# Later due times for two weight splits in a gated attention and MLP kernel on one core

## The chip, the cores and the metric

The kernel runs on one NeuronCore of a Trainium2 chip, on engines that each work through a queue of their own: TensorE (PE, matmuls, with its weight loads shown as PEld), VectorE (DVE), ScalarE (ACT), GpSimd (POOL), and SyncE (SP), which issues the DMAs. The metric is the device time of one execution in microseconds (us), as the median of several runs.

## The reference

The input x has 2048 tokens of 448 features. The result is a gated mix of a sliding-window attention and an MLP, all in float32:

```python
x = A_x
g = _sigmoid((x * gate_w).sum(-1, keepdims=True))
a = _A_ref(x, A_wqkv, A_wo)
b = _B_ref(x, B_w1, B_b1, B_w2, B_b2)
return g * a + (1 - g) * b
```

Attention has 16 heads of 28 features; each token attends to 8 earlier tokens, itself included, 2 apart. The MLP goes from 448 to 1792 features (w1), squares the positive part, and goes back to 448 (w2).

## The kernel before

**Float32 by splitting.** A matmul here multiplies in a shorter format (F32R). Every operand is split into a high part ("hi": a ScalarE copy into the shorter format) and a low part ("lo": a VectorE subtraction, raw minus hi), and a product is the sum of three matmuls, hi·hi, hi·lo and lo·hi. The weights of the MLP must be loaded, split, and kept.

**Row halves and turns.** Most matmuls use 64 rows of the array, two side by side on the two row halves, and collect in PSUM banks. When a bank has had products of one row half and is to have those of the other, something must stand between: `turn` and `turned` write one element of the bank on VectorE (lines 212 and 360), and `touch` rewrites a few weights or activations on ScalarE (line 814). Each waits for the matmuls before it, and the matmuls behind it wait for it.

**Stages.** The tokens come in four chunks of 512. The first part of the program computes q, k and v of the chunks: `qkv_first` (chunk 0, 36 full matmuls that count as 36 pairs, then 48 and 42 pairs), `qkv_two` twice for chunk 1 (63 pairs each), `qkv_seven` for chunk 2 (117 pairs in groups of three, a scheme with seven products, its banks named v, x, y, z, w), and `qkv_two` twice for chunk 3. The second call for chunk 3 has the first MLP matmuls in it (`mlp_one` behind pair 51, `mlp_two` behind pair 57). Its `run` lists the steps by pairs: 24, turn q0,k1; 30, turn q1,k0; 42, turn v0,v1; 45, evacuate q0,k1; 51, `mlp_one`; 54, evacuate q1,k0; 57, `mlp_two`; 63, evacuate v0,v1. After it the MLP runs to the end, with attention on GpSimd and VectorE beside it and its output projection in between.

**The planner.** The order of the instructions on every engine is written by hand, through a clock. `advance(dt)` adds the planned time of the matmuls just issued (203 ns for a pair of 448 columns, 227 ns for one of 512), then issues every step whose due time has come, in order of due time, and then the attention pieces that are due. `when(t, ...)` registers a step for the absolute planned time t, `at(dt, ...)` one for dt from now. `run` advances by up to 12 pairs at once; `beside` and `go` by three. So a due time says only at which of these points a step is issued. Engines execute in the order of issue: a step whose data isn't there holds all that stands behind it on its engine.

**The steps that are moved.** `w1_piece(1, dt, gap)` loads a quarter of w1 at 45,500 and splits it in four parts, part k due at dt + k·gap, with `split_full` (line 130 hi, line 131 lo 1500 ns later); the fourth part consists of four smaller ones. `w2_piece(0, 4, t, gap)` loads four of the 14 row blocks of w2 at 85,500 (the DMA is line 792) and splits block k at t + k·gap with `split_copied`: ScalarE writes hi (745) and copies the raw block to one PSUM tile named copy (746); VectorE's low (751) is due 1300 ns (COPY_DELAY) later and reads that tile, so the next block's copy waits for it. `w2_piece(4, 3, ...)` does so for three more blocks. PSUM has two rings of four banks, "m" and "b"; a new tile takes the bank that was taken longest ago, and waits until that one has been read.

Of the kernel before, what the change touches and what calls it, by code (L numbers as in the profile page):

```python
# [57 lines left out]
def gated_mix_kernel(ctx: ExitStack, tc: tile.TileContext, xT, wqkv, w1, w2, wo, b1, b2, out):  # L58
# [868 lines left out]
    def when(t, fn, *args):  # L927
        later.append((t, lambda: fn(*args)))
# [117 lines left out]
    when(10500.0, x_spill, 0, x)  # L1046
    when(25000.0, w1_piece, 0, 38000.0, 1500.0)
    when(44500.0, halos)
    when(45500.0, w1_piece, 1, 57300.0, 1200.0)
    when(66800.0, w1_piece, 2, 76300.0, 1400.0)  # L1050
    when(67800.0, w1_piece, 3, 83500.0, 900.0)
    for j in range(2):
        when(65500.0 + j * 2000.0, x_copy, 3, j)
    when(78500.0, biases)
    when(85500.0, w2_piece, 0, 4, 91000.0, 1400.0)
    when(89100.0, w2_piece, 4, 3, 99700.0, 1400.0)

    pair = {}
# [442 lines left out]
```

## Time and profile before

| | |
|---|---|
| median of 3 runs | 415.39 us (415.28 to 415.41) |
| the profiled execution | 415.74 us |
| its span, first to last instruction | 414.0 us |
| granted TensorE clock | 1.00 |
| TensorE waits inside the span, two for a turn | 2.0 and 0.7 us |
| DMA | 74.00 MB, 179 GB/s on average |

The timeline lists instructions of an engine: start (us from the start of the span), duration, engine, line of the kernel, operation, what it writes and reads, shapes, how many of them the row merges (x4), and in brackets the idle time of the engine before it and what ended that. A start may lie a little (some 0.07 us) before the end of the instruction ahead, since they overlap. The list of waits names who waited for whom, with the total, the number of times, and the longest. The list of DMA issues has the queue, the size of one and the time from issue to landing.

### The profile page before, as it was taken

The page shows a single profiled execution, that of the slowest core. Times are in us where ns is not written, and L with a number is a line of the kernel's source. Part 1 is how long each engine was busy: PE and PEld are TensorE (multiplying, and loading weights), DVE is VectorE, ACT ScalarE, POOL GpSimd, SP SyncE. Part 2 cuts the span into 40 slices and gives each one's busy share as a digit, 9 for nine tenths or more (in the row PEclk, how much of TensorE's full clock was granted, in tenths as well). Part 3 has the DMA queues.
Part 4 walks back from the last instruction along what each step waited for, and adds up shares of the span by engine and source line. Part 5 has one row for each costly group of instructions (what it writes and reads, how often), then busy time and mean ns, then how long its engine had stood idle before and what let it go on. Part 6 is the DMA issues. An engine that isn't in the chain of part 4 may idle for free.

```text
span 414.0 us, 9366 instructions
## 1 busy us (share of the span) xinstructions
PE 407.1 (98%) x3817; PEld 367.6 (89%) x3817; DVE 278.8 (67%) x454; ACT 218.5 (53%) x494; POOL 268.0 (65%) x167
## 2 busy tenths in 40 slices
PE   8999999998999999999999999999999999999997
PEld 8999998997888888888888888989898888888996
DVE  4574865483876767787665888788686676784344
ACT  4674776474775466444465525544652254346640
POOL 0000000964999999989899799899899797850000
DMA  7999799979263505554022628965155630058504
GB/s 218 346 376 332 239 367 282 368 233 332 72 211 152 207 2 180 207 186 152 2 83 76 227 97 239 254 187 155 25 170 187 228 129 0 25 138 160 127 2 179
DMA packets 67020, 74.00 MB, mean 179 GB/s; under 512 B 33504, under 2 KB 59296, under 8 KB 66848
## 3 DMA queue, kind: packets, MB, share of 16 engines
q1 hardware_dynamic: 66976, 73.39, 55.6%
q8 instruction: 30, 0.49, 0.5%
q14 instruction: 14, 0.11, 0.1%
HBM read 45.94 MB, written 28.25 MB: 179 GB/s over the span
## 4 chain that ended last, share of the span: by engine, by line
PE 95%; DMA 2%; DVE 1%; ACT 0%; issue 0%; DVEq 0%
PE b L202 32%; PE h L202 32%; PE qkv L202 14%; PE a L202 7%; DMA w2raw<-w 2%; PE v L344 2%; PE qkv L291 2%; PE x L344 1%; PE z L344 1%; PE warm L879 1%; PE a L1273 1%; PE y L344 1%; PE w L344 0%; DVE st L437 0%; DVE w17l L131 0%
## 5 line engine op out<-in xcount | busy, mean ns | idle before, releaser
L561 POOL TENSOR_TENSOR qk<-q,k 128x896 f32<-128x896 f32 x64 | 135.0, 2150 | 86.3 <-DMA k<-k_d 77.3
L568 POOL TENSOR_TENSOR av<-lg,v 128x896 f32<-128x896 f32 x64 | 119.3, 1969 | 5.1 <-DVE lg L562 4.8
L866 DVE TENSOR_TENSOR h<-h,h 128x512 fp32r<-128x512 f32 x56 | 38.5, 689 | 60.8 <-ACT h L869 60.7
L576 DVE TENSOR_REDUCE o<-av 128x112 f32<-128x896 f32 x64 | 66.7, 1074 | 0.4 <-POOL av L568 0.3
L562 DVE TENSOR_REDUCE lg<-qk 128x32 f32<-128x896 f32 x64 | 66.9, 1075 | 0.0
L202 PE MATMUL b<-w2ah,h 64*128 64x448 f32 x448 | 66.3, 359 | 0.0
L202 PE MATMUL b<-w2bh,h 64*128 64x448 f32 x448 | 66.1, 359 | 0.0
L202 PE MATMUL qkv<-wqh,x 64*128 64x448 f32 (+1 forms) x384 | 60.9, 361 | 2.0 <-DVE qkv L212 2.0
L867 ACT ACTIVATE h<-h,b1z 128x512 f32<-128x512 f32 x56 | 36.7, 656 | 42.8 <-PE h L202 42.8
L202 PEld LDWEIGHTS qkv<-wqh,x 64*128 64x128 f32 x384 | 45.4, 184 | 3.8 <-DVE qkv L212 2.3
L202 PEld LDWEIGHTS b<-w2bh,h 64*128 64x128 f32 x448 | 42.1, 184 | 3.6
L202 PE MATMUL qkv<-wql,x 64*128 64x448 f32 (+1 forms) x192 | 45.2, 361 | 0.0
L202 PEld LDWEIGHTS b<-w2ah,h 64*128 64x128 f32 x448 | 41.9, 184 | 3.7
L202 PE MATMUL b<-w2bl,h 64*128 64x448 f32 x224 | 40.6, 358 | 0.0
L202 PE MATMUL b<-w2al,h 64*128 64x448 f32 x224 | 40.5, 358 | 0.0
L868 ACT ACTIVATE h<-h 128x512 fp32r<-128x512 f32 x56 | 33.5, 599 | 1.7
L869 ACT ACTIVATE h<-h 128x512 f32<-128x512 f32 x56 | 33.2, 593 | 0.0
L814 ACT ACTIVATE h<-h 128x4 fp32r<-128x4 f32 (+1 forms) x35 | 7.2, 207 | 43.9 <-PE b L202 41.5
L243 ACT ACTIVATE st<-qkv 128x448 f32<-128x448 f32 x36 | 18.2, 542 | 16.4 <-PE qkv L202 12.9
L202 PEld LDWEIGHTS qkv<-wql,x 64*128 64x128 f32 x192 | 25.8, 185 | 0.8
L202 PEld LDWEIGHTS b<-w2bl,h 64*128 64x128 f32 x224 | 21.1, 184 | 1.9
L202 PEld LDWEIGHTS b<-w2al,h 64*128 64x128 f32 x224 | 21.0, 184 | 1.9
(263 smaller groups left out, 851.7 us busy)
## 6 DMA issues: line engine op xcount, KB each, us to landing
k<-k_d SPq DMA_DIRECT2D x8, 840.0 KB, 6.6
v<-v_d SPq DMA_DIRECT2D x8, 840.0 KB, 4.8
x_d<-x SPq DMA_DIRECT2D x12, 512.0 KB, 7.7
q_d<-st SPq DMA_DIRECT2D x8, 448.0 KB, 6.6
k_d<-st SPq DMA_DIRECT2D x8, 448.0 KB, 6.4
w1raw<-w SPq DMA_DIRECT2D x4, 896.0 KB, 10.1
q<-q_d SPq DMA_DIRECT2D x8, 448.0 KB, 3.7
o_d<-o SPq DMA_DIRECT2D x16, 224.0 KB, 2.2
```

The costliest lines, as they stand in the source:

```text
L202: nc.tensor.matmul(acc.pt[:, :acc.n], a[rows], w[rows], start=acc.todo == acc.all, stop=acc.todo == 1)
L243: nc.scalar.activation(st[:, :, t % 2], heads(pt), AF.Copy)
L291: nc.tensor.matmul(acc.pt[:, :D], a, w, start=k == j == 0, stop=False)
L344: nc.tensor.matmul(self.pt[:, :self.n], a, w, start=new, stop=True, skip_group_check=True)
L561: nc.gpsimd.tensor_mul(pr, q[:, s:s + 1].to_broadcast([P, W, C]), k[:, s:s + W])
L562: pending.append(lambda: nc.vector.tensor_reduce(lg[:, s], pr.rearrange("p w (h d) -> p w h d", h=HG), axis=AX.X, op=ALU.add))
L568: nc.gpsimd.tensor_mul(pr.rearrange("p (h d) w -> p w h d", h=HG), lg[:, s][:, :, :, None].to_broadcast([P, W, HG, DH]), v[:, s:s + W].rea ...
L576: nc.vector.tensor_reduce(o[:, g * C:(g + 1) * C], pr, axis=AX.X, op=ALU.add)
L866: nc.vector.tensor_sub(hl, pt, f32(hh))
L867: ops += [lambda pt=pt, r=r: nc.scalar.activation(pt, pt, AF.Relu, bias=b1t[:, f + r:f + r + 1]), lambda pt=pt, hh=hh: nc.scalar.activatio ...
L868: lambda pt=pt, hh=hh: nc.scalar.activation(hh, pt, AF.Square),
L869: lambda pt=pt, r=r, low=low: (nc.scalar.activation(pt, pt, AF.Square), at(delays[r], low))]
```

## The change

Two due times and gaps. The first block of the second MLP weights is split from 93,200 in steps of 1500 instead of from 91,000 in steps of 1400, and the second piece of the first MLP weights from 58,000 in steps of 1300 instead of from 57,300 in steps of 1200. The loads stay where they are, and no instruction is added or removed.

```diff
@@ -1046,13 +1046,13 @@
     when(10500.0, x_spill, 0, x)
     when(25000.0, w1_piece, 0, 38000.0, 1500.0)
     when(44500.0, halos)
-    when(45500.0, w1_piece, 1, 57300.0, 1200.0)
+    when(45500.0, w1_piece, 1, 58000.0, 1300.0)
     when(66800.0, w1_piece, 2, 76300.0, 1400.0)
     when(67800.0, w1_piece, 3, 83500.0, 900.0)
     for j in range(2):
         when(65500.0 + j * 2000.0, x_copy, 3, j)
     when(78500.0, biases)
-    when(85500.0, w2_piece, 0, 4, 91000.0, 1400.0)
+    when(85500.0, w2_piece, 0, 4, 93200.0, 1500.0)
     when(89100.0, w2_piece, 4, 3, 99700.0, 1400.0)
```

## The prediction

> **What bounds the kernel now.** I began with the engine shares, then the list of who waited for whom on TensorE.
>
> ```profile
> PE 407.1 (98%) x3817; PEld 367.6 (89%) x3817; DVE 278.8 (67%) x454; ACT 218.5 (53%) x494; POOL 268.0 (65%) x167
> ```
>
> ```profile
> PE qkv L202 <- DVE qkv L212: 2.0, 1, 2.0
> ...
> PE x L344 <- DVE w L360: 0.7, 1, 0.7
> ```
>
> TensorE sets the time. Beside its start it waits twice, each time for a VectorE memset that turns a bank: a 1x1 write to one PSUM bank, which must stand between matmuls of one row half and those of the other. The timeline of TensorE gives the places:
>
> ```profile
> 66.52 0.36 PE L344 MATMUL x<-w2ah,s_0h 64*128 64x448 f32 x1
> ...
> 70.00 0.47 PE L344 MATMUL x<-w2ah,s_0h 64*128 64x448 f32 x2 [0.65 <-DVE w L360]
> ...
> 100.85 0.36 PE L202 MATMUL qkv<-w7h,x 64*128 64x450 f32 x2
> 103.17 0.47 PE L202 MATMUL qkv<-wqh,x 64*128 64x448 f32 x2 [1.95 <-DVE qkv L212]
> 103.48 0.37 PE L202 MATMUL qkv<-wql,x 64*128 64x448 f32 x2
> ...
> 106.28 0.40 PE L202 MATMUL h<-x,w17h 64*128 64x512 f32 x2
> ...
> 110.27 0.39 PE L202 MATMUL h<-x,w1ah 64*128 64x512 f32 x2
> ```
>
> From 103.48 to 106.28 run 14 pairs, so a pair takes 2.80 / 14 = 0.20 us. Gap two: the next pair was due at 100.85 + 0.20 = 101.05 and began at 103.17, 2.12 late; the pair behind it lost 0.11 more (0.31 instead of 0.20), together **2.2 us**. Gap one: 12 pairs after 66.52 is 68.92, the start was 70.00, 1.08 late, with the same loss at the restart **1.2 us**. So 3.4 us is all that can be taken out here.
>
> **Where the edited steps stand.** The kernel's planner adds 203 ns per qkv pair and releases due steps after at most 12 pairs (3 in the third chunk and the MLP). The third chunk starts at 252 pairs, 51,156 ns; the second half of the fourth at 126 + 126 + 117 + 63 = 432 pairs, 87,696 ns. I call its points by pairs: 24 (92,568), 30 (93,786), 42 (96,222), 45 (96,831), 51 (98,049), then twelve MLP pairs of 227 ns ending at 100,773, then 54 (101,382). Banks q0,k1 are turned after 24, q1,k0 after 30, v0,v1 after 42; q0 and k1 are evacuated after 45. Before, at 24: split 0, low 0, split 1, one reduction, then the turn. VectorE shows this:
>
> ```profile
> 101.42 0.62 DVE L751 TENSOR_TENSOR w2al<-copy,w2ah 128x448 fp32r<-128x448 f32 x1 [6.84 <-ACT copy L746]
> 101.96 1.08 DVE L562 TENSOR_REDUCE lg<-qk 128x32 f32<-128x896 f32 x1
> 102.97 0.64 DVE L751 TENSOR_TENSOR w2al<-copy,w2ah 128x448 fp32r<-128x448 f32 x1
> 103.03 0.64 DVE L212 MEMSET qkv<- 1x1 f32 x4
> ...
> 104.76 2.07 DVE L562 TENSOR_REDUCE lg<-qk 128x32 f32<-128x896 f32 x2
> ```
>
> VectorE idled 6.84 us in front of low 0 with two turns queued behind it. ScalarE shows why:
>
> ```profile
> 100.37 0.58 ACT L745 ACTIVATE w2ah<-w2raw 128x448 fp32r<-128x448 f32 x1 [4.99 <-DMA w2raw<-w]
> 100.86 0.53 ACT L746 ACTIVATE copy<-w2raw 128x448 f32<-128x448 f32 x1
> 101.32 0.56 ACT L745 ACTIVATE w2ah<-w2raw 128x448 fp32r<-128x448 f32 x1
> 102.08 0.55 ACT L746 ACTIVATE copy<-w2raw 128x448 f32<-128x448 f32 x1 [0.20 <-DVE w2al L751]
> ...
> 105.37 0.96 ACT L243 ACTIVATE st<-qkv 128x448 f32<-128x448 f32 x2
> ...
> 109.25 0.21 ACT L814 ACTIVATE w1ah<-w1ah 128x2 fp32r<-128x2 f32 x1 [1.26 <-PE h L202]
> ```
>
> The split waits for the load, landed at 100.35. All splits of this piece go through one PSUM copy tile: each copy (L746) waits for the low (L751) of the row before, as at 102.08.
>
> **Part one, the second weights.** Same 4 splits and 4 lows, no new instruction, no DMA moved (the load is still released by 85,500). New due times: splits 93,200 / 94,700 / 96,200 / 97,700, lows 1300 later. Split 0 goes to point 30; low 0, split 1, low 1 and split 2 to point 42 (96,200 just makes 96,222), low 2 and split 3 to 51, low 3 into the MLP pairs. Turns q0,k1 and q1,k0 now have no low ahead, and run when their matmuls are done. The turn v0,v1 gets low 0 and low 1 ahead.
>
> So gap two goes. What is late next: **the evacuation of q0**. It stands on ScalarE behind copy 2, which waits for low 1, and the MLP's first pair needs its bank. The "m" ring has four banks; the fourth chunk takes three (q0, q1, k0), then three (q0, q1, k1), so the two MLP tiles get the older k0's bank and this q0's. The chain, from the rows above:
> - load 100.35; hi 0 100.37; copy 0 100.86 to 101.39; low 0 101.42 to 102.04 (its reduction has run long before)
> - copy 1 102.08 to 102.63; low 1, 0.03 later (as copy 1 follows low 0), 102.66 to 103.29 (no reduction stands between: those of point 42 come behind the due steps)
> - copy 2 103.32 to 103.87; evacuation of q0 from 103.80 (it overlaps by 0.06, as at 105.37), 0.54 us, to 104.34; TensorE 0.05 later, **104.39**.
>
> Before, this pair began at 106.28, on no wait. Without either gap it would come at 106.28 - 3.4 = 102.9, with gap two alone gone at 104.1. Both are ahead of 104.39, so a new wait of 0.3 to 1.5 us stands there, and the gain is 106.28 - 104.39 = 1.89, less up to 0.1 for the restart: **1.8 us**.
>
> What follows it. Turn v0,v1: low 1 to 103.29, two reductions of 1.08, so 105.4; needed 9 pairs of this mix behind 104.39, at about 107.7: covered. The ScalarE touch of line 814, which frees the second MLP pass: low 2 to 105.8, copy 3 to 106.4, a reduction to 106.8, low 3 to 107.4, the next piece's copy to 108.0, touch to 108.15. TensorE wants it at 110.27 - 1.89 = 108.38: covered by 0.2 us only. If that cover fails the gain is what is left of 110.27 - 108.15 = 2.1, so each further reduction in this queue would cost 1.08 - 0.2 = 0.9 us.
>
> The load's landing is the anchor. It is issued at 90.74 behind a key load that waits for GpSimd, not TensorE:
>
> ```profile
> 90.74 0.39 SPq L792 DMA_DIRECT2D w2raw<-w  x1
> ...
> 95.80 1.20 SPq L792 DMA_DIRECT2D w2raw<-w  x1
> ```
>
> ```profile
> w2raw<-w SPq DMA_DIRECT2D x1, 896.0 KB, 9.6
> ...
> w2raw<-w SPq DMA_DIRECT2D x1, 672.0 KB, 10.2
> ...
> q_d<-st SPq DMA_DIRECT2D x1, 448.0 KB, 8.9
> ```
>
> If gap one goes, the stores of q and k behind the load are issued 1.2 us earlier. At worst they take half of the transfer for that time, and it lands 0.6 us later; at best nothing changes. The q store landed at about 92.7 + 8.9 = 101.6, behind the load, which is nearer to no change; I take 0 and keep 0.6 for the range.
>
> The Trainium skill, page "DMA: Bandwidth & Descriptors", section "Queues, rings and completion order", says that each DMA engine consumes the descriptors of one issuing queue in ring order, and that completion is nevertheless not first-in, first-out. By ring order the sum stays at 1.8, by free interleaving it would be 1.2; the landings at 100.35 and 101.6 agree with the first.
>
> **Part two, the first weights.** Old and new due times of the four splits: 57,300 / 58,500 / 59,700 / 60,900 and 58,000 / 59,300 / 60,600 / 61,900; lows 1500 behind the point of release. Before, the last low (four pieces) came ahead of the turn of x:
>
> ```profile
> 66.43 0.63 DVE L131 TENSOR_TENSOR w1al<-w1raw,w1ah 128x448 fp32r<-128x448 f32 x1 [1.13 <-ACT w1ah L130]
> 66.98 1.15 DVE L437 TENSOR_TENSOR st<-y,st 128x448 f32<-128x448 f32 x2
> 68.04 0.61 DVE L131 TENSOR_TENSOR w1al<-w1raw,w1ah 128x448 fp32r<-128x448 f32 x1
> 68.69 1.17 DVE L131 TENSOR_TENSOR w17l<-w1raw,w17h 64x64 fp32r<-64x64 f32 x4
> 69.86 0.06 DVE L360 MEMSET x<- 1x1 f32 x2
> ```
>
> ```profile
> 64.96 0.98 ACT L433 ACTIVATE st<-x 128x448 f32<-128x448 f32 x2 [0.79 <-DMA q_d<-st]
> 65.82 1.05 ACT L130 ACTIVATE w1ah<-w1raw 128x448 fp32r<-128x448 f32 x2
> 66.89 1.26 ACT L130 ACTIVATE w17h<-w1raw 64x64 fp32r<-64x64 f32 x4
> 68.06 0.95 ACT L433 ACTIVATE st<-z 128x448 f32<-128x448 f32 x2
> ```
>
> After, low 2 is released at 62,727 ahead of the turn of x and low 3 at 63,945 behind it, ahead of the turn of w. ScalarE: hi 1 and hi 2 still at 65.82, then the evacuation of z, now ahead of the four pieces: at 67.1 at the earliest, at 68.06 as before at the latest (it had no wait there). VectorE: the two adds start between 65.94 (x evacuated) and 66.98 as before, I take 66.4; 1.15 later low 1, then low 2 to 68.7, turn of x at 68.7; with the late end 69.3, which would leave 0.4 us of gap one. TensorE needs it at 68.92: gap one goes, with 0.2 us to spare. Turn of w: the pieces end 0.95 + 1.26 behind the start of z's evacuation, at 69.3 to 70.3, low 3 0.3 later; needed 9 pairs behind 68.92, at 70.7, so covered by 0.1 us at least. The raw buffer is released at 69.6 to 70.6 instead of 69.86; the load that waits for it on SP's queue is split some 20 us later. It all gives 1.2 us to TensorE at 70, which **wait again at 104.39**, because that chain hangs on a landing: I cost part two at 0 in the sum. Were the evacuation not in the way, it would be worth its 1.2.
>
> **Behind 110 us.** TensorE has no wait there, so it carries the gain on unless something not tied to it is late. GpSimd:
>
> ```profile
> 97.47 2.13 POOL L561 TENSOR_TENSOR qk<-q,k 128x896 f32<-128x896 f32 x1
> 103.12 2.13 POOL L561 TENSOR_TENSOR qk<-q,k 128x896 f32<-128x896 f32 x1 [3.52 <-DVE qkv L212]
> ```
>
> It waited for the reduction behind low 0. That reduction now runs ahead of the lows, so the product starts at 97.47 + 2.13 = 99.6. The mask step behind it waits for the first of the two reductions that stood at 104.76 (end 105.80) and now follow low 1 (end 104.3): it comes 1.5 us earlier, close to TensorE's 1.8. The last projection reads of attention are landed long before their split:
>
> ```profile
> 369.90 1.38 SPq L1205 DMA_DIRECT2D ot<-o_d  x2
> ```
>
> ```profile
> DMA to landing us min/median/max: 2.8/3.5/5.9
> ```
>
> ```profile
> 380.12 0.83 ACT L1222 ACTIVATE oh<-ot 128x768 fp32r<-128x768 f32 x1
> ```
>
> At the longest landing of such reads (the second fence) the data is there at 371.3 + 5.9 = 377.2, 2.9 us ahead of the split. On ScalarE the splits of piece two press on the MLP's first evacuations and the touch near 115; I see 0 to 0.2 us there and leave it in the range.
>
> **The sum**: 1.8 us. The profiled execution took 415.74 us (span 414.0), the median of the runs shown is 415.39; taken off the median, 415.39 - 1.8 = **413.6 us**; 413.9 with a span of 412.2 for the profiled one.
>
> **Rivals.**
> - *The bank isn't held*, or the chain is quicker than I have it. Then the touch bounds (2.1 us, 413.3), or in the extreme both gaps go whole (3.4 us, 412.0). For it: no row shows a wait for q0's evacuation yet. Against it: the order on ScalarE follows from the due times, and both bounds hang on the same landing.
> - *The queue fills again*: the landing comes 0.6 later and one more reduction (0.9) falls ahead of the touch: 1.8 - 0.6 - 0.9 = 0.3 us, 415.1, which is within 0.2% (0.8 us, about what a measurement of this kernel can tell from no change). For it: covers of 0.2 us.
> - *Slower*: ScalarE stands in front of the touch with the first split of piece two, whose load landed at 95.80 + 10.2 = 106.0. A hi, a copy and the touch behind it take about 1.35 us. If the load lands behind 108.9, the second MLP pass starts later than 110.27, microsecond for microsecond: a landing at 110 would give 416.5. For it: stores issued earlier share its transfer. Against: it needs 2.9 us more than before.
> - *The edits don't move what they say* (released at the same points): 415.4. Excluded by the due times above, but for an error in my count.
>
> **How the numbers follow.** Forecast 0.56, with its own range from 1.2 (late landing) to 2.0 us, 413.4 to 414.2. Bank not held, 0.16 (about 0.10 near 413.3, the rest down to 412.0). Queue fills again, 0.16; 0.04 of it still is a gain over 0.8 us. Slower, 0.07. Edit without effect, 0.05. Faster 0.56 + 0.16 + 0.04 = 0.76; same 0.12 + 0.05 = 0.17; slower 0.07. A range of 412.8 to 415.0 leaves out 0.05 below and some 0.14 above.
>
> **What would show it.** Right: the wait for L212 gone; q turns near 99; a new TensorE wait at the first h matmul for ScalarE's evacuation (L243), h near 104.4; the x turn ahead of 69; nothing new behind 110. Wrong: h without a wait, a wait of the second pass for L814, or a landing off 100.35.

## The result and the profile after

| | before | after |
|---|---|---|
| median of 6 runs | 415.33 us (415.01 to 415.55) | 412.94 us (412.59 to 413.50) |
| profiled execution, span | 415.74 us, 414.0 us | 412.90 us, 411.1 us |

The ratio after to before is 0.9943, with a 95% interval of 0.993 to 0.9956, so 1.8 to 2.9 us faster. The forecast was 413.6 in a range of 412.8 to 415.0.

The waits of TensorE in the profile after, in all, times, longest:

```profile
PE warm L879 <- DVE b1z L877: 1.2, 1, 1.2
PE qkv L291 <- DVE x L909: 0.4, 1, 0.4
```

Both are at the start. The two waits for a turn (L212 and L360) are gone, and no wait has come in their place. The predicted one, at the first MLP pair, isn't in the list. The timelines of ScalarE, VectorE and TensorE at that place, in this order, show how near it was:

```profile
99.36 0.58 ACT L745 ACTIVATE w2ah<-w2raw 128x448 fp32r<-128x448 f32 x1 [4.67 <-DMA w2raw<-w]
...
102.30 0.55 ACT L746 ACTIVATE copy<-w2raw 128x448 f32<-128x448 f32 x1 [0.20 <-DVE w2al L751]
102.79 0.96 ACT L243 ACTIVATE st<-qkv 128x448 f32<-128x448 f32 x2
...
106.88 0.19 ACT L814 ACTIVATE w1ah<-w1ah 128x2 fp32r<-128x2 f32 x1
```

```profile
95.72 0.14 DVE L212 MEMSET qkv<- 1x1 f32 x2 [0.73 <-PE qkv L202]
98.15 0.14 DVE L212 MEMSET qkv<- 1x1 f32 x2 [2.29 <-PE qkv L202]
100.40 0.62 DVE L751 TENSOR_TENSOR w2al<-copy,w2ah 128x448 fp32r<-128x448 f32 x1 [2.11 <-ACT copy L746]
101.64 0.62 DVE L751 TENSOR_TENSOR w2al<-copy,w2ah 128x448 fp32r<-128x448 f32 x1 [0.62 <-ACT copy L746]
102.18 2.07 DVE L562 TENSOR_REDUCE lg<-qk 128x32 f32<-128x896 f32 x2
...
104.25 0.06 DVE L212 MEMSET qkv<- 1x1 f32 x2
```

```profile
103.16 0.37 PE L202 MATMUL qkv<-wqh,x 64*128 64x448 f32 x2
103.36 0.51 PE L202 MATMUL h<-x,w17h 64*128 64x512 f32 x2
```

The turns of q0,k1 and q1,k0 now wait for TensorE alone, ahead of every low. The evacuation of q0 stands behind copy 2, as predicted, and ends at 102.79 + 0.53 = 103.32; the MLP pair that needs its bank begins at 103.36, which is also its place in the beat of 0.20 us. The chain from the load took 103.36 - 99.34 = 4.02 us, against 4.04 in the prediction. What differs is the landing, 99.34 instead of 100.35, and TensorE's own arrival (taken up below). So in this execution the new bound was reached and not passed, and the first MLP pair came 106.28 - 103.36 = 2.92 us earlier.

That is more than the mechanism gives. Two profiled executions with landings 1.0 us apart can't say what the edit is worth; the experiments are for that.

### The profile page after: what moved, and what is told of

Read it like the earlier page. It is cut to its first block, busy times and chain, and to the rows that moved or that the text cites. A ratio compares the mean times of both kernels' runs of the same rounds, so it can differ in the third digit from the quotient of the medians.

```text
span 411.1 us, 9365 instructions
## 1 busy us (share of the span) xinstructions
PE 406.5 (99%) x3817; PEld 398.4 (97%) x3817; DVE 278.8 (68%) x454; ACT 218.0 (53%) x494; POOL 267.8 (65%) x167
## 4 chain that ended last, share of the span: by engine, by line
PE 98%; DMA 1%; DVE 0%; SPq 0%; issue 0%
PE b L202 33%; PE h L202 32%; PE qkv L202 17%; PE a L202 7%; PE v L344 2%; PE qkv L291 2%; PE x L344 1%; PE z L344 1%; PE a L1273 1%; DMA xraw<-xT 1%; PE y L344 1%; PE w L344 1%; PE last L1273 0%; DVE bt L1152 0%; SPq L886 0%; PE last L1265 0%
## 5 line engine op out<-in xcount | busy, mean ns | idle before, releaser
L202 PE MATMUL b<-w2ah,h 64*128 64x448 f32 x448 | 71.9, 359 | 0.0
L202 PEld LDWEIGHTS b<-w2ah,h 64*128 64x128 f32 x448 | 50.8, 184 | 0.0
L202 PEld LDWEIGHTS b<-w2bh,h 64*128 64x128 f32 x448 | 50.5, 184 | 0.0
L202 PE MATMUL b<-w2al,h 64*128 64x448 f32 x224 | 46.8, 358 | 0.0
L202 PE MATMUL b<-w2bl,h 64*128 64x448 f32 x224 | 46.7, 358 | 0.0
L202 PEld LDWEIGHTS qkv<-wqh,x 64*128 64x128 f32 x384 | 36.5, 184 | 2.5
L202 PE MATMUL qkv<-wql,x 64*128 64x448 f32 (+1 forms) x192 | 35.2, 360 | 0.0
L202 PEld LDWEIGHTS b<-w2al,h 64*128 64x128 f32 x224 | 27.3, 184 | 0.0
L202 PEld LDWEIGHTS b<-w2bl,h 64*128 64x128 f32 x224 | 27.1, 184 | 0.0
L202 PEld LDWEIGHTS qkv<-wql,x 64*128 64x128 f32 x192 | 18.4, 184 | 1.3
```

The costliest lines, as they stand in the source:

```text
L202: nc.tensor.matmul(acc.pt[:, :acc.n], a[rows], w[rows], start=acc.todo == acc.all, stop=acc.todo == 1)
```

## The experiments

Theory A: before, the turn, and after, the evacuation of q0, hang on the load's landing, at fixed distances. Rivals: the two gaps add without a bound behind them (B); only the place of the steps behind the turns counts (C); each later rival is named with its run, and A' in the last runs is A with a first gap of 0.36 us. In each table row the ratio is to the kernel before on the same chip, with its 95% interval. Where the diffs show one line, it is the changed line against the kernel before, except where said.

**One edit at a time.**

```diff
-    when(85500.0, w2_piece, 0, 4, 91000.0, 1400.0)
+    when(85500.0, w2_piece, 0, 4, 93200.0, 1500.0)
```

> Only the second weights' edit. Theory A (the evacuation of q0, anchored on the landing of the load, bounds the first MLP pair at landing + 4.0 us): the first gap of 1.2 us stays at about 69, the wait for the turn (L212) at 101 goes, and the first MLP matmul comes about 2.2 us earlier than in the kernel before, at or within 0.3 us of where the evacuation ends; 413.1 us, close to the changed kernel's 412.9. Rival B (the two gaps simply add, nothing bounds behind them): 415.3 - 2.2 = 413.1 too, but no closeness to the evacuation, and 1.2 us slower than with both edits.

```diff
-    when(45500.0, w1_piece, 1, 57300.0, 1200.0)
+    when(45500.0, w1_piece, 1, 58000.0, 1300.0)
```

> Only the first weights' edit. Theory A (TensorE waits again for a chain that hangs on the load's landing): the gap at 69 goes, the wait for the turn (L212) near 100 grows from 2.2 to about 3.4 us, and the time stays at 415.3, within 0.3 us. Rival B (gaps add): 414.1.

| | median | ratio |
|---|---|---|
| second weights alone (12 runs) | 413.17 us | 0.9936 (0.9908 to 0.9964) |
| first weights alone (12 runs) | 415.30 us | 0.9995 (0.9963 to 1.0028) |
| kernel before (35 runs) | 415.23 us | |

The second weights' edit alone gives the gain. With the first alone the median does not move, as A says, but its interval also holds B's 414.1, so the times alone do not decide between them; the rows do. TensorE and ScalarE with the first weights' edit alone:

```profile
99.64 0.36 PE L202 MATMUL qkv<-w7h,x 64*128 64x450 f32 x2
102.67 0.48 PE L202 MATMUL qkv<-wqh,x 64*128 64x448 f32 x2 [2.67 <-DVE qkv L212]
```

```profile
99.88 0.58 ACT L745 ACTIVATE w2ah<-w2raw 128x448 fp32r<-128x448 f32 x1 [5.71 <-DMA w2raw<-w]
```

The first gap is gone, and TensorE waits longer at the second: the load landed at 99.86, and the matmul behind the turn began 2.81 later. Before it was 103.17 - 100.35 = 2.82. What was won at the first gap was waited away at the second, as A says. I had expected a gap of 3.4 us; with a landing 0.5 earlier it is 2.8.

With the second weights' edit alone the first MLP pair began at 103.08, without a wait, 0.13 behind the end of the evacuation and 3.2 us earlier than in the first profile of the kernel before (I had expected 2.2); the load landed 1.38 earlier than there. The first gap, with the old order of the first weights, was not the 1.2 us that I expected:

```profile
66.45 0.36 PE L344 MATMUL x<-w2ah,s_0h 64*128 64x448 f32 x2
...
69.09 0.48 PE L344 MATMUL x<-w2ah,s_0h 64*128 64x448 f32 x2
```

The 12 pairs between take 2.40, so 0.24 us are lost, and 0.12 at the restart, 0.36 together.

**The evacuation put behind all four splits** (against the changed kernel; the turns keep their place ahead of every low).

```diff
-    when(85500.0, w2_piece, 0, 4, 93200.0, 1500.0)
+    when(85500.0, w2_piece, 0, 4, 92600.0, 1400.0)
```

> The changed kernel with the second weights' first piece due at 92600 in steps of 1400: the turns of q0,k1 and q1,k0 still have no low ahead, but all four splits stand ahead of the evacuation of q0 on ScalarE. Theory A: the evacuation now waits behind copy 3, which waits for low 2 behind two reductions, so TensorE waits some 2.5 us at the first MLP pair for ScalarE (L243); 415.2 to 415.5. Rival C (only the place behind the turns counts): 412.9, no wait at the MLP pair.

416.66 us, ratio 1.0024 (0.9985 to 1.0063): the whole gain is lost although the turns stand as in the changed kernel. Rival C falls, and with the wait below the prediction's rival that the bank isn't held. ScalarE and TensorE:

```profile
105.10 0.55 ACT L746 ACTIVATE copy<-w2raw 128x448 f32<-128x448 f32 x1 [1.51 <-DVE w2al L751]
105.59 0.96 ACT L243 ACTIVATE st<-qkv 128x448 f32<-128x448 f32 x2
```

```profile
103.83 0.39 PE L202 MATMUL h<-x,w17h 64*128 64x512 f32 x1
106.17 0.79 PE L202 MATMUL h<-x,w17h 64*128 64x512 f32 x1 [1.94 <-ACT st L243]
```

The matmul at 103.83 is one half of the first MLP pair; the other half, which needs q0's bank, starts at 106.17, 0.05 behind the end of q0's evacuation (105.59 + 0.53 = 106.12). The time came out 1.2 to 1.5 us above the 415.2 to 415.5 expected. A lower clock is at work there: the matmul took 0.79 us instead of 0.39, and the five of the ten runs with a mean granted clock of 0.996 have a median of 418.2 us, the five at 1.00 one of 415.4. The clock is taken up below.

**The landing moved**, with the splits left alone. First the kernel before, with the load ahead of the next unit's q and k loads on SP's queue:

```diff
-    when(85500.0, w2_piece, 0, 4, 91000.0, 1400.0)
+    when(85000.0, w2_piece, 0, 4, 91000.0, 1400.0)
```

> The kernel before with the load of the second weights' first piece released at 85000 instead of 85500, ahead of the next unit's q and k loads on SP's queue; the splits stay where they were. Theory A (the landing is the anchor): landing 3 to 5 us earlier, at 95.5 to 97.5, the wait for the turn at 101 goes without any split being moved, the first gap of 1.2 us stays; 413.1. Rival C (the order on VectorE counts, not the landing): 415.3.

413.22 us, ratio 0.9935 (0.9906 to 0.9963): as much as the whole change, without any split moved. The load was issued at 88.39 and took 4.9 us instead of 9.6, so it landed at 93.3, earlier than the 95.5 to 97.5 expected. The first split, in its old place, no longer waits for it:

```profile
94.70 0.58 ACT L745 ACTIVATE w2ah<-w2raw 128x448 fp32r<-128x448 f32 x1
```

TensorE's list has no wait behind its start. The first gap, which I had again expected at 1.2 us, was 0.23 and 0.11 at the restart. So the order on VectorE did harm only because the data was late.

Then the changed kernel with the load behind the stores of q and k:

```diff
-    when(85500.0, w2_piece, 0, 4, 93200.0, 1500.0)
+    when(86000.0, w2_piece, 0, 4, 93200.0, 1500.0)
```

> The changed kernel with the load released at 86000, behind the stores of q and k on SP's queue. Theory A: landing 1.5 to 3 us later, 101 to 102.5; the first MLP pair waits for ScalarE (L243) and begins at landing + 4.05 us, 105 to 106.5 instead of 103.4; 414.6 to 416, and more if the granted clock drops behind the wait. Rival F (the evacuation of q0 doesn't bound): 412.9 with no such wait.

```profile
102.82 0.58 ACT L745 ACTIVATE w2ah<-w2raw 128x448 fp32r<-128x448 f32 x1 [8.39 <-DMA w2raw<-w]
...
106.24 0.96 ACT L243 ACTIVATE st<-qkv 128x448 f32<-128x448 f32 x2
```

```profile
103.10 0.39 PE L202 MATMUL h<-x,w17h 64*128 64x512 f32 x1
106.82 0.50 PE L202 MATMUL h<-x,w17h 64*128 64x512 f32 x1 [3.33 <-ACT st L243]
```

Landing 102.80, MLP pair at 106.82: 4.02 behind it. This is the predicted wait at its predicted distance from the landing. The median is 417.58 us, ratio 1.005 (1.002 to 1.0081), 3 to 1.6 us more than the 414.6 to 416 that I gave for the wait alone. Two of the ten runs kept a mean clock of 1.00 and took 416.0 and 416.4 us; the clock adds to the other eight (below).

**Both kernels again, and the early load on the changed kernel.**

> The changed kernel again, for the spread of its landing and of its gaps, beside the kernel before on the same chip. Theory A: landing of the load between 98.9 and 100.4; the first MLP pair no earlier than landing + 4.0 us; where the landing is behind 99.4 a wait for ScalarE (L243) shows, below that none; 412.9, granted clock 1.00, and a smaller spread than the kernel before. Rival D (the first weights' edit is worth 1.2 us): clearly faster than the second edit alone (413.2), by about 1 us.

> The kernel before again, for a second profile of its two gaps. Theory A: the turn's memset at landing + 2.7 us, whatever the landing is; the first gap between 0 and 1.2 us, with the landing of the q store that ScalarE's evacuation of x waits for; where the second gap is over 2.3 us the granted clock drops behind it for some us. Rival G (the clock drop has to do with the chip only, not with the gap): a drop with a short gap too, or elsewhere in the span.

```diff
-    when(85500.0, w2_piece, 0, 4, 93200.0, 1500.0)
+    when(85000.0, w2_piece, 0, 4, 93200.0, 1500.0)
```

> The changed kernel with the load released at 85000, ahead of the next unit's q and k loads. Theory A: landing near 94.6, the evacuation of q0 ends as soon as the pairs are done, about 102.8; TensorE had no wait left in the changed kernel's profile, so the time stays at 412.9, within 0.3 us. Rival E (late landings still cost the changed kernel something in most executions): 0.3 to 0.6 us faster.

| | median | ratio |
|---|---|---|
| changed kernel again (12 runs) | 413.02 us | 0.9943 (0.9922 to 0.9964) |
| changed, early load (12 runs) | 412.69 us | 0.993 (0.9906 to 0.9954) |
| kernel before again (10 runs) | 414.58 us | 0.999 (0.9956 to 1.0025) |
| kernel before (35 runs) | 414.96 us | |

The profile of the changed kernel run again shows the new wait with the load at its own place:

```profile
99.70 0.58 ACT L745 ACTIVATE w2ah<-w2raw 128x448 fp32r<-128x448 f32 x1 [5.54 <-DMA w2raw<-w]
...
103.13 0.96 ACT L243 ACTIVATE st<-qkv 128x448 f32<-128x448 f32 x2
```

```profile
102.83 0.39 PE L202 MATMUL h<-x,w17h 64*128 64x512 f32 x1
103.71 0.50 PE L202 MATMUL h<-x,w17h 64*128 64x512 f32 x1 [0.48 <-ACT st L243]
```

Landing 99.68, pair at 103.71, again 4.03. And the kernel before, with an early landing:

```profile
101.76 0.47 PE L202 MATMUL qkv<-wqh,x 64*128 64x448 f32 x2 [1.19 <-DVE qkv L212]
104.88 0.39 PE L202 MATMUL h<-x,w17h 64*128 64x512 f32 x2
```

```profile
98.97 0.58 ACT L745 ACTIVATE w2ah<-w2raw 128x448 fp32r<-128x448 f32 x1 [4.23 <-DMA w2raw<-w]
```

Here the landing is 98.95, the turned pair 2.81 behind it, and the MLP pair 104.88 - 98.95 = **5.93** behind it. In the first profile of the kernel before it was 106.28 - 100.35 = 5.93 too.

**The four combinations of the first weights' edit and the early load on one chip**, each with the second weights' edit.

> The second weights' edit and the early load (85000), without the first weights' edit. Theory A': with the early load nothing holds TensorE at the first MLP pair, so the first gap, 0.36 us in the profiles of the old order (0.24 and 0.12 at the restart), is not given back: 0.3 to 0.4 us slower than the same with both edits; 413.0 if the other is 412.7. Rival B (the first gap is 1.2 us as in the first profile): 1.2 us slower.

> Both edits and the early load again, on the same chip as the run without the first weights' edit: 412.7, no wait of TensorE behind its start.

> The changed kernel on the same chip: 0.1 to 0.4 us above the one with the early load, by the executions in which the landing comes behind 99.3 and the evacuation of q0 holds the first MLP pair; a landing of 99.7 would show a wait for L243 of about 0.4 us.

> The second weights' edit alone on the same chip. Theory A': within 0.2 us of the changed kernel, since the first gap's 0.36 us is mostly given back where the evacuation of q0 bounds. Rival B: 1.2 us above it.

| | load as before | load early |
|---|---|---|
| second weights only | 413.79 us, 0.9968 (0.9951 to 0.9984) | 412.86 us, 0.9957 (0.9935 to 0.998) |
| both edits | 413.00 us, 0.9948 (0.993 to 0.9967) | 412.75 us, 0.995 (0.9931 to 0.9969) |

The kernel before stood at 414.81 us there. With the second weights' edit alone and the load as before, the wait for the evacuation shows again:

```profile
100.62 0.58 ACT L745 ACTIVATE w2ah<-w2raw 128x448 fp32r<-128x448 f32 x1 [5.54 <-DMA w2raw<-w]
```

```profile
104.63 0.49 PE L202 MATMUL h<-x,w17h 64*128 64x512 f32 x1 [0.48 <-ACT st L243]
```

What the first weights' edit is worth is not settled: 0.79 us with the load as before, where I had expected under 0.2, and 0.11 with the early load, where I had expected 0.3 to 0.4. The intervals against the kernel before overlap in each column. Set against each other, the left column still differs: eight of the twelve runs without the edit are slower than all nine with it. That is more than the gap of 0.36 us in the profiles, and its cause stays open. Both columns lie below 1.2 us; the run with that edit alone can't tell, since its interval holds 1.2 us. With the early load the changed kernel is 0.25 to 0.33 us lower in both comparisons, inside their spread, and TensorE has no wait behind its start in those two profiles; it has the lowest median here, by a difference that isn't shown.

## Why the prediction was right, step by step

**The new bound and its size: right.** Four profiles in which TensorE reached it, the first without a wait, the other three with one:

| kernel | landing | MLP pair | distance |
|---|---|---|---|
| changed, first profile | 99.34 | 103.36 | 4.02 |
| changed, again | 99.68 | 103.71 | 4.03 |
| second weights only, last run | 100.60 | 104.63 | 4.03 |
| changed, load late | 102.80 | 106.82 | 4.02 |

Against 5.93 for the kernel before, so the edit is worth 5.93 - 4.03 = **1.90 us** wherever both hang on the landing, whatever that is. This is the predicted 1.89. It is why the forecast held although its anchor didn't: a late landing delays both kernels alike. Where the load lands early the changed kernel keeps its own beat and the distance is longer: with the second weights' edit alone and a landing at 98.97 the pair came at 103.08, 4.11 behind it, without a wait. On the two chips on which the changed kernel ran again the medians differ by 414.96 - 413.02 = 1.94 and 414.81 - 413.00 = 1.81. Without the runs at a mean clock of 0.996 or less, which only the kernel before has, it is 1.76 and 1.75.

The number itself was in part luck. The first comparison gave 2.39 us, above the 1.2 to 2.0 of the forecast itself, and 412.94 lies below its 413.4 to 414.2, among the times that the prediction had given to the rival that the bank isn't held. The interval of 1.8 to 2.9 holds 1.9. Two of the three signs that the prediction had named for being wrong came in the first profile: the first MLP pair without a wait, and a landing off 100.35.

**The landing as a fixed time: wrong.** The prediction took 100.35 from one execution and let it vary only by what the change does to it. In nine profiles with the load at its place it lay between 98.95 and 100.60. So "a new wait of 0.3 to 1.5 us stands there" was right in its place, but was 0, 0.5 and 0 us in the three profiles of the changed kernel, not the 1.5 that both gaps removed would leave at 100.35. In the first of them the landing came 1.01 earlier than before, and TensorE was 0.49 late from its start, most of it a wait for its first tokens (L291 in the list above). Its first pair on row halves, before and after:

```profile
12.61 0.48 PE L202 MATMUL qkv<-w7h,x 64*128 64x448 f32 x2
```

```profile
13.10 0.48 PE L202 MATMUL qkv<-w7h,x 64*128 64x448 f32 x2
```

Together these 1.5 us are the whole of the missing wait: 106.28 - 3.4 + 0.49 = 103.37, where the pair began. So in that execution both gaps went in full, which the prediction had only under a rival.

The feared delay by the earlier stores doesn't show: the load took 9.4 us from issue to landing after the change and 9.6 before. With 8.2 to 10.0 in all nine profiles, a delay of 0.6 us would not stand out, and it is not excluded. The Trainium skill, page "DMA: Bandwidth & Descriptors", section "Queues, rings and completion order", has each DMA engine consume one queue's descriptors in ring order; the runs with the load moved on SP's queue agree, with 4.9 us when it stood ahead of the q and k loads.

**The first gap: mis-sized.** The term of 1.2 us was that of one execution. ScalarE's evacuation of x waited there until 64.96 for the q store to land; in the second profile of the kernel before it began at 64.23 and the gap was 0.24 us and the loss at the restart. With the new order it was 0 in every profile. Its place in the sum, 0, rests on a TensorE that waits again further on. That is so in the run with this edit alone (0.9995), and in the changed kernel only where it waits for the evacuation; beside the second edit its worth stays open between 0.1 and 0.8 us.

**The covers: right.** The turn of v0,v1 ran at 104.25 (landing + 4.9; predicted 5.0), and the touch of line 814 ended at 107.07 (landing + 7.7; predicted 7.8), 0.27 us ahead of the second MLP pass at 107.34, where the prediction had 0.2. GpSimd's mask step began at 103.34 instead of 105.92, 2.6 us earlier, of which 1.0 is the landing. No wait came behind 110 us.

**The rivals.** That the bank isn't held fell with the evacuation put late. That the queue fills again, and that the second piece's load holds the touch, did not occur: its first split began at 105.34 without waiting for a DMA. That the edits don't move what they say is excluded by the order of the memsets and lows above.

**What was missing: the clock.** The prediction priced a gap at its length. The windows of the run with the first weights' edit alone show more (the columns: window, its length, busy time and number of instructions of PE, PEld, DVE, ACT and POOL, granted TensorE clock, DMA share, GB/s):

```profile
103.00:104.00 1.00, 1.00 (x12) 0.95 (x10) 0.45 (x4) 0.86 (x2) 1.00 (x1) 0.95 0.51 186
104.00:105.00 1.00, 1.00 (x8) 0.88 (x7) 1.00 (x2) 0.74 (x2) 0.74 (x1) 0.50 0.08 30
105.00:106.00 1.00, 1.00 (x8) 0.88 (x8) 1.00 (x2) 0.54 (x2) 0.58 (x1) 0.50 0.01 2
106.00:107.00 1.00, 1.00 (x8) 0.91 (x6) 1.00 (x5) 0.96 (x4) 1.00 (x2) 0.50 0.02 8
107.00:108.00 1.00, 1.00 (x10) 0.87 (x8) 1.00 (x2) 0.49 (x1) 1.00 (x1) 0.84 0.00 0
```

Soon after the wait of 2.67 us the granted clock halves; 0.05 + 3 x 0.50 + 0.16 = 1.7 us of full clock are lost, which is 0.4% of the execution and makes a mean clock of 0.996. A loss of the same size shows in the run with the evacuation put late (last section). It strikes some executions and not others. The mean clock was 0.996 or less in 24 of 109 timed runs of the kernel before (8 of 35, 10 of 35 and 3 of 10, 3 of 29) and in 5 of the 12 with the first weights' edit alone, and in none of 94 runs of the kernels whose second gap is removed. Their times are higher by more than one such loss: on the chip of the first experiments the median of the 8 was 418.5 us, that of the other 27 was 414.9; what the rest of that difference is, no run here shows. So the change takes away these executions besides its own gain. Means tell that (415.7 before and 413.2 after on the second chip, 2.5 us apart), medians hardly.

## What to carry to other kernels

A step whose data comes by DMA should stand on no in-order queue ahead of something that the bottleneck engine needs, and a move past one such thing brings it before the next: ask what on the other engine of the pair is now behind it (here ScalarE's evacuation behind the copies). Measure the bound as a distance from the event that it hangs on (landing + 4.0 against landing + 5.9), since the event moved by more than a microsecond from execution to execution here, and the distance by hundredths. Where a chain starts with a load, try first whether the load can be issued earlier: that alone gave the whole gain.

## What the hardware showed unexpectedly

- **TensorE waits of 1.94 and 2.67 us were followed by half the granted clock for 3.4 us.** After the wait of 2.67 us the missing clock adds up to 1.7 us at 0.50, which makes 3.4 us of half clock; in the run with the evacuation put late the wait was 1.94 us, and its windows show the same:

```profile
106.00:107.00 1.00, 0.83 (x4) 0.74 (x6) 1.00 (x2) 1.00 (x4) 1.00 (x2) 0.60 0.03 8
107.00:108.00 1.00, 1.00 (x6) 0.75 (x6) 1.00 (x2) 0.45 (x2) 1.00 (x1) 0.50 0.00 0
108.00:109.00 1.00, 1.00 (x8) 0.76 (x6) 1.00 (x3) 0.00 (x0) 0.32 (x1) 0.50 0.00 0
109.00:110.00 1.00, 1.00 (x10) 0.82 (x8) 0.34 (x1) 0.00 (x0) 0.59 (x1) 0.70 0.00 0
```

  But the clock stayed at 1.00 behind the wait of 3.33 us in the profile with the late load, while 8 of the 10 timed runs of that kernel had a mean clock of 0.996 or less; and it did behind the wait of 1.95 us in the first profile of the kernel before. So length alone doesn't decide. The Trainium skill, page "TensorE: Matmul & The Clock Gate", section "What's actually happening", describes a clock gate that halves the clock after an idle window of about 3.4 us and gives it back after a busy one of the same length, in windows that run free of the kernel. The half rate agrees with the runs, and the 3.4 us with the time until the full clock came back; the waits in front of it were shorter than an idle window of that length. A window that runs free of the kernel could be why the same wait strikes only at times; no run here tests it. The same page of the Trainium skill, section "Why this matters for your kernels", gives idle gaps over some 3 us as the ones to avoid; here the half clock came behind waits of 1.94 and 2.67 us.
- **Landings vary.** The same 896 KB load, at the same place of its queue, landed between 98.95 and 100.60 us after the start in nine executions. Its issue lay between 89.92 and 90.81, the time from issue to landing between 8.2 and 10.0 us, so the larger part of the spread is in the latter. The latest issue of the nine (90.81) had one of the earliest landings (98.99).
